# A DiT block on one core: summing a gate vector over partition quadrants by copies, and regrouping the K projection around its scale groups

## The chip, the core and the metric

The kernel runs on one core of one Trainium2 chip. The metric is the device time of one execution in microseconds; the time before is the median of five executions. A profile of one execution stands beside it. Engines are named as the profile names them: PE (matrix multiply), PEld (its weight loads), DVE (vector engine), ACT (scalar engine), POOL (GpSimd), SP (sync engine, which here only issues DMAs).

## The reference, cut to what matters

```python
B, N, D = x.shape            # 2, 256, 1152 ; F = 4 * D ; H = 2 heads of 576
mod = (_silu(c) @ w_mod).reshape(B, 6, 1, D)
shift_a, scale_a, gate_a, shift_m, scale_m, gate_m = [mod[:, i] for i in range(6)]
h = _layernorm(x, axis=-1) * (1 + scale_a) + shift_a
qkv = (h @ wqkv).reshape(B, N, 3, H, Dh)
# ... attention over 256 tokens, softmax, a = attention @ wo
x = x + gate_a * a
h2 = _layernorm(x, axis=-1) * (1 + scale_m) + shift_m
m = _gelu(h2 @ w_fc1) @ w_fc2
return x + gate_m * m
```

All inputs are bfloat16. Two pieces matter here: `1 + scale_a`, which multiplies the normalised x before the K projection, and `gate_m`, a vector of 1152 numbers for each of the two samples, which multiplies the result of the MLP at the very end.

## The kernel before, in words

The 512 tokens (`T`, two samples of `N` = 256) lie as four tiles of 128 rows. D = 1152 is nine blocks of 128 (`KD`), F = 4608 is 36 (`KF`). All matrix products accumulate in PSUM tiles with the tag "acc", of which there are six; smaller PSUM results use the tag "aux", of which there are two. Weights go through five large SBUF buffers (the pool "wide"), loaded by SP in the order in which the code names them. At the end of the program every instruction is chained to the one before it on its own engine (lines 820 to 830), so each engine executes exactly in the order in which the code is written; engines meet only through semaphores.

The parts that the change touches are these.

**The K projection, lines 376 to 410.** `k_step(k, c0, c1, m0, m1)` multiplies block k of the modulated input `hT0` with the weight blocks m0 to m1 - 1 of `w_k`, for token columns c0 to c1; six output blocks (`KM1`) accumulate side by side in the six "acc" tiles while k runs from 0 to 8. Steps 0, 1 and 2 are done in halves of 256 tokens, one half for each sample; steps 3 to 8 take all 512 columns in one matmul for each output block. Ahead of step k + 1, `transpose_x` turns block k + 1 of the normalised x with four PE transposes into an aux tile, and `both` multiplies it with the scale: DVE takes sample 0 (the first 256 columns), ACT takes sample 1 (the other 256). The scale itself comes from `scale_group(k0, k1)`: nine matmuls with two columns for each block, out of `w_scale_a`, which arrives by DMA in five pieces (`SGROUPS`: blocks 0-1, 2-3, 4-5, 6-7, 8), each followed by the piece of `w_k` that goes with it. The groups for blocks 4-5, 6-7 and 8 are computed inside steps 3, 5 and 7. In steps 3 and 5, `split` says how many of the six matmuls of the step are issued ahead of the scale group; the rest follow after the group and the transposes.

**The gate of the MLP.** `gate_vector(1, w_gate_m)` is called after output block m = 22 of the first MLP product (line 784). On DVE it multiplies each of the nine row blocks of the gate weights with the sample's silu(c), one number for each partition, and adds them up in `part` (lines 468 to 476). What remains is a sum over the 128 partitions. DVE's 32 x 32 block transpose and a reduction (lines 477 to 483) sum over the 32 partitions of each quadrant and leave `folded`: in quadrant a, partition 32a + r holds the quadrant's partial sums of columns 32j + r. `gate_vector_finish`, called after m = 34 (`KF - 2`, line 786), adds the four quadrants and turns the result: two matmuls in fp32 with the constant 0/1 matrix `fold` (built at line 454), one for each sample. DVE casts the 36 x 64 result to bfloat16, POOL writes it to DRAM (`gates_dram`, line 495), and `broadcast_gate` (line 460) reads it back into all 128 partitions as `gate`.

**The second MLP product, lines 800 to 817.** Thirteen groups, each 36 matmuls into an "acc" tile; DVE then multiplies with the gate (line 812, the first reader of `gate_m`), POOL adds x1, SP writes the rows out.

Of the kernel before, what the change touches and what calls it, by code (L numbers as in the profile page):

```python
# [8 lines left out]
FP32 = mybir.dt.float32  # L9
BF16 = mybir.dt.bfloat16  # L10
ACT = mybir.ActivationFunctionType
ALU = mybir.AluOpType
AX = mybir.AxisListType
# [6 lines left out]
def kernel(  # L20
# [11 lines left out]
    nc = tc.nc  # L32
    B, N, D = x.shape
# [3 lines left out]
    P = 128  # L37
    T = B * N
# [3 lines left out]
    KF = F // P  # L42
# [10 lines left out]
    const = ctx.enter_context(tc.tile_pool(name="const", bufs=1))  # L53
    act = ctx.enter_context(tc.tile_pool(name="act", bufs=1))
    wide = ctx.enter_context(tc.tile_pool(name="wide", bufs=5))
    work = ctx.enter_context(tc.tile_pool(name="work", bufs=2))
    small = ctx.enter_context(tc.tile_pool(name="small", bufs=4))
    psum = ctx.enter_context(tc.tile_pool(name="psum", bufs=2, space=PSUM))

    def acc_tile(shape, name, dt=FP32):  # L60
        return psum.tile(shape, dt, name=name, tag="acc", bufs=6)

    def aux_tile(shape, name, dt=FP32):
        return psum.tile(shape, dt, name=name, tag="aux", bufs=2)
# [27 lines left out]
    ident = const.tile([P, P], BF16, name="ident")  # L92
# [26 lines left out]
    def load_rows(name, view, col0):  # L119
        w = wide_tile(name)  # L120
        for r in range(0, KD, 3):
            load = nc.sync.dma_start(w[:, r:r + 3, :], view[:, r:r + 3, col0:col0 + D])
            first_load.setdefault(name, load.ins)
        return w
# [118 lines left out]
    def scale_group(k0, k1, tile_of=aux_tile, pm=None):  # L243
        if pm is None:
            pm = tile_of([P, k1 - k0, B], "pm")
        for j in range(k0, k1):
            if j == 0:
                nc.tensor.matmul(pm[:, 0, :], ones_row[:], ones_row[:, 0:B], start=True, stop=False)
            for k in range(KD):
                nc.tensor.matmul(  # L250
                    pm[:, j - k0, :], w_scale_a[:, k, j * P:(j + 1) * P], sT[:, k, 0:B],
                    start=(k == 0 and j > 0), stop=(k == KD - 1),
                )
        return pm

    def scale_add(pm, k0, k1, eng="d"):
        if eng == "a":
            nc.scalar.activation(scale_a[:, k0:k1, :], pm[:], ACT.Identity, bias=ones[:])
        else:
            nc.vector.tensor_scalar_add(scale_a[:, k0:k1, :], pm[:], 1.0)  # L260

    def transpose_x(ks, ts, pt=None, j0=0):
        if pt is None:
            pt = aux_tile([P, len(ks), len(ts) * P], "pt", BF16)
        for j, t in enumerate(ts, j0):
            for i, k in enumerate(ks):
                nc.tensor.transpose(pt[:, i, j * P:(j + 1) * P], xns[t][:, k * P:(k + 1) * P], ident[:])
        return pt
# [9 lines left out]
    def k_step(k, c0=0, c1=T, m0=0, m1=KM1):  # L278
        for m in range(m0, m1):
            if k == 0 and c0 == 0:  # L280
                pk[m] = acc_tile([P, T], "pk")
            nc.tensor.matmul(  # L282
                pk[m][:, c0:c1], w_k[:, k, m * P:(m + 1) * P], hT0[:, k, c0:c1],
                start=(k == 0 and c0 == 0), stop=(k == KD - 1), skip_group_check=True,
            )
# [33 lines left out]
    def both(pt, k):  # L319
        for b, e in enumerate("da"):  # L320
            modulate(pt, 0, k, b, b * N, e)
# [76 lines left out]
    k_step(2, 0, N)  # L398
    k_step(2, N, T)
    for k in range(3, KD):  # L400
        split = 2 if k in (3, 5) else 0
        k_step(k, 0, T, 0, split)
        if k in (3, 5, 7):
            k1 = min(k + 3, KD)
            scale_add(scale_group(k + 1, k1), k + 1, k1)
        if k < KD - 1:
            both(transpose_x([k + 1], range(NT)), k + 1)
        k_step(k, 0, T, split)
    for m in range(KM1):
        k_evac(m)  # L410

# [38 lines left out]

    s32 = const.tile([P, KD, B], FP32, name="s32")
    nc.vector.tensor_copy(s32[:], sT[:, :, 0:B])
    fold = const.tile([P, 32], FP32, name="fold")
    nc.vector.tensor_reduce(fold[:], ident[:].rearrange("p (q a) -> p a q", a=32), axis=AX.X, op=ALU.add)
    gates_dram = tc.dram_tile([2, B, D], BF16, name="gates_dram")

    def broadcast_gate(g):
        gate = act.tile([P, B, D], BF16, name="gate", tag="gate")
        for b in range(B):
            nc.gpsimd.dma_start(gate[:, b, :], gates_dram[g, b:b + 1, :].partition_broadcast(P))  # L460
        return gate
# [3 lines left out]
    def gate_vector(g, wg):  # L465
        part = act.tile([P, B, D], FP32, name="part", tag="x_sb")
        folded = small.tile([P, B, D // 32], FP32, name="folded", tag="folded", bufs=1)
        for k in range(KD):
            for b in range(B):
                if k == 0:  # L470
                    nc.vector.tensor_scalar_mul(part[:, b, :], wg[:, k, :], s32[:, k, b:b + 1])  # L471
                else:
                    nc.vector.scalar_tensor_tensor(  # L473
                        part[:, b, :], wg[:, k, :], s32[:, k, b:b + 1], part[:, b, :],
                        op0=ALU.mult, op1=ALU.add,
                    )
        for b in range(B):
            for c in range(0, D, PW):
                blocks = work.tile([P, PW // 32, 32], FP32, name="tmp", tag="tmp", bufs=3)
                nc.vector.transpose(blocks[:].rearrange("p j r -> p (j r)"), part[:, b, c:c + PW])  # L480
                nc.vector.tensor_reduce(
                    folded[:, b, c // 32:(c + PW) // 32], blocks[:], axis=AX.X, op=ALU.add
                )

        return lambda: gate_vector_finish(g, folded)

    def gate_vector_finish(g, folded):
        rows = D // 32
        pg = aux_tile([rows, B, 32], "pg")
        for b in range(B):  # L490
            nc.tensor.matmul(pg[:, b, :], folded[:, b, :], fold[:], start=True, stop=True)
        nat = work.tile([rows, B, 32], BF16, name="nat_v", tag="nat_v", bufs=1)
        nc.vector.tensor_copy(nat[:], pg[:])  # L493
        for b in range(B):
            nc.gpsimd.dma_start(gates_dram[g, b, :].rearrange("(j r) -> j r", r=32), nat[:, b, :])  # L495
        return broadcast_gate(g)

    def gate_natural(g, wg):
# [130 lines left out]
    w_gate_m = load_rows("w_gate_m", wmod_v, S_GATE_M * D)  # L629
# [106 lines left out]
    def load_f2(j):  # L736
        w = wide.tile([P, 27, PW], BF16, name=f"w_f2_{j}", tag="wide")
        i = 27 * j
        while i < 27 * (j + 1):
            n, kk = divmod(i, KF)  # L740
            cnt = min(KF - kk, 27 * (j + 1) - i)
            nc.sync.dma_start(w[:, i - 27 * j:i - 27 * j + cnt, :], wfc2_v[:, kk:kk + cnt, n * PW:(n + 1) * PW])
            i += cnt
        w_f2.append(w)
# [3 lines left out]
    def f1_mm(dst, m, k, c0, c1, start, **kw):  # L748
        ml = m % KD
        nc.tensor.matmul(  # L750
            dst, w_f1[m // KD][:, k, ml * P:(ml + 1) * P], hT[:, k, c0:c1],
            start=start, stop=(k == KD - 1), **kw,
        )
# [23 lines left out]
    gate_m = None  # L777
    for m in range(MSPLIT, KF):
        pacc = acc_tile([P, T], "pacc")
        for k in range(KD):  # L780
            f1_mm(pacc[:], m, k, 0, T, k == 0)
        nc.scalar.activation(gT[:, m, :], pacc[:], ACT.Gelu_apprx_tanh)  # L782
        if m == 22:
            gate_m_finish = gate_vector(1, w_gate_m)
        if m == KF - 2:
            gate_m = gate_m_finish()
        if m == MSPLIT:
            load_f2(0)
        if m > MSPLIT and m % KD == KD - 1:
            load_f2(m // KD)  # L790
# [9 lines left out]
    for gi, (n, t, c0, cw) in enumerate(groups):  # L800
        b = t // TPB
        last = gi == len(groups) - 1
        pacc = acc_tile([P, cw], "pacc")
        for kk in range(KF):
            j, r = divmod(n * KF + kk, 27)
# [3 lines left out]
                start=(kk == 0), stop=(kk == KF - 1),  # L809
# [51 lines left out]
```

## Time and profile before

| what | value |
|---|---|
| median of five executions | 243.68 us (243.43 to 244.09) |
| the profiled execution, its own time | 243.68 us |
| its span (first to last instruction in the profile) | 241.9 us |
| PE busy | 235.6 us, 97% of the span |
| DVE, ACT, POOL busy | 38%, 25%, 12% of the span |
| granted PE clock | 1.00 throughout |
| DMA traffic | 53.30 MB, mean 220 GB/s |

How to read it: a row of the chain of waits or of the timeline begins with the start in us from the start of the span and a length in us. "x18" is the number of instructions merged into the row. In the timeline the end of a matmul is modelled and includes the time in the pipeline, so the rows of PE overlap; a row of n matmuls that follow each other is as long as n - 1 distances from start to start and one duration. In the chain of waits the pieces do not overlap. A bracket at the end of a timeline row is the idle time of that engine just before, and what ended it. Time to landing of a DMA is counted from its issue.

### The profile page before, as it was taken

To read this page: it belongs to the slowest core of one execution; us is meant where nothing else is said; L and a number is where in the kernel's file an instruction comes from. 1 tells how busy PE (TensorE), PEld (TensorE's weight loads), DVE (VectorE), ACT (ScalarE), POOL (GpSimd) and SP (SyncE) were. 2 spreads that over 40 slices of the span, in tenths; PEclk is the share of its full clock that TensorE was granted. 3 is DMA by queue.
4 is the path that set the end of the run, shared out by engine and by line. 5 is a ranking of instruction groups with operands and counts; after the bars stand their busy time and mean duration, and the time that the engine had idled before them with its cause. 6 is when DMAs were issued, how large, how long until landed. Compare 5 with 4: busy or idle time off the path is not lost.

```text
span 241.9 us, 3993 instructions
## 1 busy us (share of the span) xinstructions
PE 235.6 (97%) x1698; PEld 144.1 (60%) x1698; DVE 91.5 (38%) x194; ACT 60.1 (25%) x122; POOL 28.3 (12%) x47
## 2 busy tenths in 40 slices
PE   8799999999999999999999999999999999999994
PEld 6575444466667666888844444444666566665674
DVE  4842442319325678831002999960010000000001
ACT  6732322307215032671422333322000000000000
POOL 2300000002300323200000000001121111111111
PEclk9999999999999999999999999999999999999999
DMA  6999999996599993739999999999300000000000
GB/s 213 327 315 310 377 366 392 390 391 224 106 327 394 390 290 76 194 60 354 390 390 393 340 327 289 265 326 294 98 16 16 20 16 16 19 18 16 25 26 16
DMA packets 48925, 53.30 MB, mean 220 GB/s; under 512 B 9731, under 2 KB 36619, under 8 KB 48907
## 3 DMA queue, kind: packets, MB, share of 16 engines
q1 hardware_dynamic: 41312, 50.14, 62.2%
q10 hardware_dynamic: 7083, 1.72, 4.4%
q0 software_dynamic: 512, 1.19, 1.9%
q8 instruction: 13, 0.21, 0.4%
q14 instruction: 5, 0.04, 0.1%
HBM read 50.15 MB, written 1.19 MB: 212 GB/s over the span
## 4 chain that ended last, share of the span: by engine, by line
PE 91%; SPq 4%; DMA 4%; issue 0%; DVE 0%; DVEq 0%
PE pacc L806 29%; PE pacc L750 29%; PE pacc L697 7%; PE pacc L603 7%; PE pq L525 7%; DMA w_scale_a<-in_w_mod_dram 4%; SPq L106 3%; PE pk L311 2%; PE pk L282 2%; PE pa L644 2%; PE ps_s L560 2%; PE pn L420 2%; SPq L88 1%; SPq L109 1%; PE pg L502 0%; PE pm L250 0%
## 5 line engine op out<-in xcount | busy, mean ns | idle before, releaser
L750 PE MATMUL pacc<-hT,w_f 128*128 128x256 bf16 (+1 forms) x432 | 70.5, 326 | 0.0
L806 PE MATMUL pacc<-w_f,gT 128*128 128x384 bf16 (+2 forms) x468 | 70.5, 314 | 0.0
L806 PEld LDWEIGHTS <-gT 128*128 128x128 bf16 x468 | 44.4, 98 | 26.3
L750 PEld LDWEIGHTS <-w_f 128*128 128x128 bf16 x432 | 42.2, 98 | 27.6
L812 DVE TENSOR_TENSOR tmp<-pacc,gate 128x384 f32<-128x384 f32 (+2 forms) x13 | 6.9, 527 | 65.6 <-PE pacc L806 57.1
L782 ACT ACTIVATE gT<-pacc 128x512 bf16<-128x512 f32 x24 | 14.3, 597 | 32.6 <-PE pacc L750 32.6
L473 DVE SCALAR_TENSOR_TENSOR part<-w_gate_m,s,part 128x1152 f32<-128x1152 bf16 x16 | 21.4, 1412 | 0.0
L814 POOL TENSOR_TENSOR o_sb<-tmp,x 128x384 bf16<-128x384 f32 (+1 forms) x12 | 11.7, 972 | 53.9 <-DVE tmp L812 53.9
L697 PE MATMUL pacc<-w_o,big 128*128 128x384 bf16 x108 | 17.9, 326 | 0.0
L525 PE MATMUL pq<-hT,w_q 128*128 128x512 bf16 x81 | 17.8, 379 | 0.0
L603 PE MATMUL pacc<-w_v,hT 128*128 128x384 bf16 x108 | 17.7, 326 | 0.0
L603 PEld LDWEIGHTS <-hT 128*128 128x128 bf16 x108 | 10.5, 98 | 7.1 <-issue 0.3
L697 PEld LDWEIGHTS <-big 128*128 128x128 bf16 x108 | 10.4, 98 | 7.2 <-issue 0.4
L525 PEld LDWEIGHTS <-w_q 128*128 128x128 bf16 x81 | 7.8, 98 | 9.4
L282 PE MATMUL pk<-big,w_k 128*128 128x256 bf16 (+1 forms) x72 | 13.2, 325 | 0.0
L703 POOL TENSOR_TENSOR x<-tmp,x_sb 128x384 f32<-128x384 f32 x8 | 7.3, 912 | 27.1 <-DMA w_scale_m<-in_w_mod_dram 15.2
L471 DVE TENSOR_SCALAR part<-w_gate_m,s 128x1152 f32<-128x1152 bf16 x2 | 1.6, 819 | 22.1 <-DMA w_gate_m<-in_w_mod_dram 22.1
L495 POOL DMA_DIRECT2D gates_dram<-nat_v x2 | 1.1, 534 | 67.7 <-DVE nat_v L493 67.7
L282 PEld LDWEIGHTS <-w_k 128*128 128x128 bf16 x72 | 6.8, 97 | 3.5 <-issue 0.2
L771 ACT ACTIVATE gT<-pacc 128x512 bf16<-128x512 f32 x12 | 6.5, 598 | 9.1 <-PE pacc L750 9.1
L516 POOL DMA_DIRECT2D gates_dram<-nat x4 | 2.3, 583 | 49.7 <-DVE nat L513 49.1
L702 DVE TENSOR_TENSOR tmp<-pacc,gate 128x384 f32<-128x384 f32 x12 | 6.6, 548 | 3.1 <-PE pacc L697 3.1
(106 smaller groups left out, 163.3 us busy)
## 6 DMA issues: line engine op xcount, KB each, us to landing
w_f<-in_w_fc_dram SPq DMA_DIRECT2D x12, 864.0 KB, 14.4
w_f<-in_w_fc_dram SPq DMA_DIRECT2D x3, 1728.0 KB, 10.0
w_f<-in_w_fc_dram SPq DMA_DIRECT2D x2, 2592.0 KB, 17.3
w_gate_a<-in_w_mod_dram SPq DMA_DIRECT2D x3, 864.0 KB, 12.7
w_v<-in_wqkv_dram SPq DMA_DIRECT2D x3, 864.0 KB, 13.8
w_o<-in_wo_dram SPq DMA_DIRECT2D x3, 864.0 KB, 14.0
w_shift_m<-in_w_mod_dram SPq DMA_DIRECT2D x3, 864.0 KB, 8.4
w_scale_m<-in_w_mod_dram SPq DMA_DIRECT2D x3, 864.0 KB, 14.8
```

The lines of the kernel that those rows point to most:

```text
L106: nc.sync.dma_start(w_k[:, k0:k1, c0:c1], wqkv_v[:, k0:k1, D + c0:D + c1])
L282: nc.tensor.matmul(pk[m][:, c0:c1], w_k[:, k, m * P:(m + 1) * P], hT0[:, k, c0:c1], start=(k == 0 and c0 == 0), stop=(k == KD - 1), skip_g ...
L473: nc.vector.scalar_tensor_tensor(part[:, b, :], wg[:, k, :], s32[:, k, b:b + 1], part[:, b, :], op0=ALU.mult, op1=ALU.add,)
L525: nc.tensor.matmul(pq[m][:], w_q[:, k, m * P:(m + 1) * P], hT[:, k, :], start=(k == 0), stop=(k == KD - 1), skip_group_check=True,)
L603: nc.tensor.matmul(pacc[:], hT[:, k, t * P:(t + 1) * P], w_v[:, k, pnl * PW:(pnl + 1) * PW], start=(k == 0), stop=(k == KD - 1),)
L697: nc.tensor.matmul(pacc[:], aT[:, k, t * P:(t + 1) * P], w_o[:, k, c0:c1], start=(k == 0), stop=(k == KD - 1),)
L703: (nc.gpsimd if pool_add else nc.vector).tensor_tensor(x1[:, t, c0:c1], tmp[:], x_sb[:, t, c0:c1], op=ALU.add)
L750: nc.tensor.matmul(dst, w_f1[m // KD][:, k, ml * P:(ml + 1) * P], hT[:, k, c0:c1], start=start, stop=(k == KD - 1), **kw,)
L782: nc.scalar.activation(gT[:, m, :], pacc[:], ACT.Gelu_apprx_tanh)
L806: nc.tensor.matmul(pacc[:], gT[:, kk, t * P:(t + 1) * P], w_f2[j][:, r, c0 - n * PW:c0 - n * PW + cw], start=(kk == 0), stop=(kk == KF - 1),)
L812: nc.vector.tensor_tensor(tmp[:], pacc[:], gate_m[:, b, c0:c0 + cw], op=ALU.mult)
L814: (nc.vector if last else nc.gpsimd).tensor_tensor(o_sb[:], tmp[:], x1[:, t, c0:c0 + cw], op=ALU.add)
```

## The change

Two parts of the code are changed.

In the K projection, three instead of two of the six matmuls of steps 3 and 5 are issued ahead of the scale group. Steps 4 and 6 are done in two halves of 256 columns, first the six matmuls of sample 0, then the six of sample 1.

In the gate of the MLP, the two fp32 matmuls with `fold` are gone, and so is `fold`. In their place POOL copies the four partition quadrants of `folded` by four DMAs from SBUF to SBUF side by side onto 32 partitions (`quads`); DVE sums the four with one reduction into `total`, a tile of 32 x 96 that is cleared first, turns it with a 32 x 32 block transpose, and casts it to bfloat16. Two DMAs write the result to DRAM, and the broadcast is as before. All of this is now issued in one go from `gate_vector` after m = 22; nothing is left after m = 34.

```diff
@@ K projection
     for k in range(3, KD):
-        split = 2 if k in (3, 5) else 0
+        split = 3 if k in (3, 5) else 0
         k_step(k, 0, T, 0, split)
         if k in (3, 5, 7):
             k1 = min(k + 3, KD)
             scale_add(scale_group(k + 1, k1), k + 1, k1)
         if k < KD - 1:
             both(transpose_x([k + 1], range(NT)), k + 1)
-        k_step(k, 0, T, split)
+        for c0, c1 in ((0, N), (N, T)) if k in (4, 6) else ((0, T),):
+            k_step(k, c0, c1, split)
...
-    fold = const.tile([P, 32], FP32, name="fold")
-    nc.vector.tensor_reduce(fold[:], ident[:].rearrange("p (q a) -> p a q", a=32), axis=AX.X, op=ALU.add)
...
@@ gate_vector
-        return lambda: gate_vector_finish(g, folded)
-
-    def gate_vector_finish(g, folded):
         rows = D // 32
-        pg = aux_tile([rows, B, 32], "pg")
-        for b in range(B):
-            nc.tensor.matmul(pg[:, b, :], folded[:, b, :], fold[:], start=True, stop=True)
-        nat = work.tile([rows, B, 32], BF16, name="nat_v", tag="nat_v", bufs=1)
-        nc.vector.tensor_copy(nat[:], pg[:])
-        for b in range(B):
-            nc.gpsimd.dma_start(gates_dram[g, b, :].rearrange("(j r) -> j r", r=32), nat[:, b, :])
+        quads = small.tile([32, P // 32, B * rows], FP32, name="quads", tag="quads", bufs=1)
+        for a in range(P // 32):
+            nc.gpsimd.dma_start(quads[:, a, :], folded[32 * a:32 * (a + 1), :, :].rearrange("p b j -> p (b j)"))
+        total = small.tile([32, 96], FP32, name="total", tag="total", bufs=1)
+        nc.vector.memset(total[:], 0.0)
+        nc.vector.tensor_reduce(
+            total[:, 0:B * rows], quads[:].rearrange("p a c -> p c a"), axis=AX.X, op=ALU.add,
+        )
+        turned = small.tile([32, 96], FP32, name="turned", tag="turned", bufs=1)
+        nc.vector.transpose(turned[:], total[:])
+        nat = small.tile([32, 96], BF16, name="nat_v", tag="nat_v", bufs=1)
+        nc.vector.tensor_copy(nat[:], turned[:])
+        flat = gates_dram[g, :, :].rearrange("b (j r) -> (b j) r", r=32)
+        nc.gpsimd.dma_start(
+            flat[0:64, :].rearrange("(q c) r -> c q r", q=2), nat[:, 0:64].rearrange("c (q r) -> c q r", q=2),
+        )
+        nc.gpsimd.dma_start(flat[64:B * rows, :], nat[0:B * rows - 64, 64:96])
         return broadcast_gate(g)
...
@@ first MLP product
         if m == 22:
-            gate_m_finish = gate_vector(1, w_gate_m)
-        if m == KF - 2:
-            gate_m = gate_m_finish()
+            gate_m = gate_vector(1, w_gate_m)
```

## Prediction

> **What bounds the kernel now.** I read the page first: which engine is busy, and what ended last.
>
> ```profile
> PE 235.6 (97%) x1698; PEld 144.1 (60%) x1698; DVE 91.5 (38%) x194; ACT 60.1 (25%) x122; POOL 28.3 (12%) x47
> ...
> PE 91%; SPq 4%; DMA 4%; issue 0%; DVE 0%; DVEq 0%
> ```
>
> PE makes up 91% of the chain that ended last, so an edit can pay only if it takes instructions off PE or shortens a stretch in which PE stands still. The other engines have more than half of their time free. Next I read the chain of waits in order of time, to see where it leaves PE.
>
> ```profile
> 10.98 8.70 DMA w_scale_a<-in_w_mod_dram
> 19.68 0.04 issue
> 19.73 0.60 PE pm L250 x18
> ...
> 21.44 0.22 PE pt L267 x4
> 21.66 1.34 PE pk L282 x6
> ...
> 97.95 68.26 PE pacc L750 x423
> 166.21 0.26 PE pg L491 x4
> 166.46 2.05 PE pacc L750 x9
> 168.51 70.31 PE pacc L806 x468
> ```
>
> Up to 19.68 us the end is set by SP's queue and one transfer: the piece of `w_scale_a` for blocks 6-7, issued at 10.98, landed 8.70 us later. From 19.73 on PE runs to the last groups with no piece of another engine in between. So a PE instruction saved after 19.73 moves the end by its full length, as long as no landing or release comes up behind it; PE time saved before 19.73 gains nothing, it only lengthens the wait there. The four `pg` pieces (two fp32 matmuls, executed as four passes) are on that chain. The waits of PE confirm the one late DMA:
>
> ```profile
> PE pm L250 <- DMA w_scale_a<-in_w_mod_dram: 0.6, 1, 0.6
> ```
>
> The timeline around this wait (step 5 with its group, then step 6), with one earlier row of half-width matmuls:
>
> ```profile
> 10.06 1.03 PE L282 MATMUL pk<-big,w_k 128*128 128x256 bf16 x8
> ...
> 17.27 1.89 PE L282 MATMUL pk<-big,w_k 128*128 128x512 bf16 x8
> ...
> 20.64 0.35 DVE L273 TENSOR_SCALAR big<-pt,scale_a 128x256 bf16<-128x256 bf16 x1
> ...
> 21.03 0.47 ACT L274 ACTIVATE big<-pt,scale_a 128x256 bf16<-128x256 bf16 x1 [2.75 <-DVE big L273]
> ...
> 21.28 0.39 PE L267 MATMUL pt<-ident,xn 128*128 128x128 bf16 x4
> ...
> 21.55 1.46 PE L282 MATMUL pk<-big,w_k 128*128 128x512 bf16 x6
> ```
>
> See three things. The eight matmuls from 17.27 start every (1.89 - 0.38)/7 = 0.216 us (0.38 is one duration), so PE is out of work at 17.27 + 8 x 0.216 = 19.00 and stands until 19.73: 0.73 us (the page counts 0.58, from the modelled end). ACT begins only when DVE has finished its half, and ends at 21.50. Step 6 starts at 21.55, 0.27 after the transposes before it, where other steps start 0.22 after theirs: about 0.05 us of waiting for ACT that the page does not list.
>
> Last, the timeline at the gate:
>
> ```profile
> 164.30 0.60 ACT L782 ACTIVATE gT<-pacc 128x512 bf16<-128x512 f32 x1 [1.34 <-PE pacc L750]
> 166.13 0.33 PE L491 MATMUL pg<-fold,folded 128*36 128x32 f32 x4
> 166.24 0.60 ACT L782 ACTIVATE gT<-pacc 128x512 bf16<-128x512 f32 x1 [1.35 <-PE pacc L750]
> ...
> 168.54 0.60 ACT L782 ACTIVATE gT<-pacc 128x512 bf16<-128x512 f32 x1 [1.71 <-PE pacc L750]
> 171.48 1.11 POOL L460 DMA_DIRECT2D gate<-gates_dram  x2 [3.41 <-DMA gates_dram<-nat_v]
> 175.24 0.56 DVE L812 TENSOR_TENSOR tmp<-pacc,gate 128x384 f32<-128x384 f32 x1 [8.53 <-DMA gate<-gates_dram]
> ```
>
> Gelu follows each output block, so its starts are a clock for PE: 1.94 us from block to block, but 2.30 us over the block with `pg` in front. The gate arrives at 175.24 and its first reader waits for it, without hurting PE.
>
> **The change part by part.**
>
> *The fp32 matmuls go.* By the clock of the gelus they cost 2.30 - 1.94 = 0.36 us of PE; by their pieces in the chain, 0.26. I take 0.36, since it also holds what the switch between data types costs around them. Nothing takes their place on PE. Gain 0.36.
>
> *The new path of the gate.* `folded` is done at 160.99 (the last reduction starts at 160.43 and takes 0.56). POOL followed DVE's cast by 0.29 us before, so the first copy is issued at 161.28; at 0.53 us for an issue (row of L495) the fourth goes at 162.87. The trace has no copy from SBUF to SBUF of this kind. The nearest row is the write of `nat_v`: 3.5 to 3.9 us to landing while weights stream; all DMAs with `gates_dram` lie between 1.6 and 5.2. I take 3.7, landing at 166.6. DVE then reduces 288 numbers (row of L481: 0.55 for 384), transposes 96 columns (L425: 0.32 for 128) and casts (0.22): about 1.1 with handover; the memset runs while the copies fly. At 167.7 + 0.29 = 168.0 POOL issues two writes, the second at 168.5, landing at 172.0 by 3.5; the broadcast is issued 0.43 later, as before, and the gate is there 3.76 after that: 176.2, one microsecond later than before. With 1.6 for both steps it would be 172, with 5.2 for those and the broadcast 181. Here a rule of the Trainium skill reads otherwise: "DMA: Bandwidth & Descriptors", Anatomy of one DMA, gives a DMA from POOL a fixed cost of about 2.0 us, most of it the wait for the write's receipt. By it the copies land at 164.9 and the writes 1.5 us sooner after their issue: an estimate of 173. Both cost nothing, because PE does not wait for the gate: six accumulators are there, a group takes 70.31/12 = 5.86 us, so the seventh group at 168.3 + 6 x 5.86 = 203.5 is the first that needs the accumulator of the first. The cover is 22 us beyond the slow bound; gone, each microsecond over it would cost one.
>
> *Queues that this is moved past.* Issued at m = 22 instead of 34, the path adds four POOL issues (2.1 us) to four that stay, and on DVE a memset, a reduction and a transpose. DVE has nothing of its own between 160.99 and the first product with the gate; what stands behind the new wait on DVE is the gate's own path and L812, which needs the gate anyway. POOL has nothing between 99.3 and its first addition behind L812. SP's loads of `w_fc2` wait for none of these; the last was issued at 154.6, ahead of the copies, which move 37 KB against megabytes. ACT gets nothing. The fold constant at 33.44 took DVE 0.36 us ahead of 4.76 us of idle time: 0.
>
> *Three matmuls ahead of the group.* In step 5 the ninth matmul fills 0.216 of the 0.73 us of standing still. The landing is not touched: up to it SP issues the same transfers, which wait for no engine. So the group starts at 19.73 as before, and 0.216 us less work stands behind it. Gain 0.216. It shrinks once the landing comes over 0.51 us sooner, is gone at 0.73, and stays 0.216 if the landing is late. In step 3 the same move only shifts work about, with the group's weights present: 0, ahead of the wait anyway.
>
> *The price: less cover for the scaling.* Three matmuls instead of four now stand between the transposes of block 6 and those of block 7. Block 7's transposes start at 20.41 + 3 x 0.216 = 21.06, and step 6 could start at 21.28; ACT ends at 21.50. Undivided, step 6 would lose the 0.216 just won. Divided, its first half needs only DVE's part, ready at 20.99 (0.29 of slack), and its second half starts at 21.28 + 6 x 0.109 = 21.93 (0.43 of slack to ACT). So nothing waits, and the old 0.05 goes too. Step 4 works alike, before the wait: 0.
>
> *Halving a step.* Half-width matmuls start every (1.03 - 0.27)/7 = 0.109 us in steps 0 and 1. Twelve of them take 1.31 against six at 0.216, 1.30: +0.01 to +0.02 in step 6. A rule of the Trainium skill speaks against this: "TensorE: Matmul & The Clock Gate", Back-to-back issue gap, says that in a real stream of weight loads and matmuls the spacing is set by both, and gives about 81 ns at 128 columns and 131 at 512. Linear between them, 256 columns would be about 98 ns (an estimate), and halving would cost 12 x 98 - 6 x 131 = 0.39 us for step 6, turning the gain of the K part into a loss of 0.12 (0.27 - 0.39), in all 243.4. The row decides: this stream is at 216 ns for 512 columns, so width sets the spacing, and the weight load of 98 ns still fits into 109. The other formula of that section, N/2.4 + 2.5 ns, gives 109.
>
> *Sum.* -0.36 - 0.216 - 0.05 + 0.02 = -0.61 us. The profiled execution took 243.68 us with a span of 241.9; the 1.78 outside stays. It equals the median of the five runs, so the sum stands against both: 243.1 us.
>
> *What comes next.* With PE earlier by 0.25 after step 6, landings get nearer: the piece for block 8 lands at 14.02 + 8.0 = 22.0, wanted at 22.63 before; the last panel of `w_k` at 17.05 + 8.2 = 25.25, wanted at 25.67; `w_shift_a` at 18.51 + 10.8 = 29.31, wanted at 29.86. The smallest slack is 0.42, so 0.17 is left.
>
> **The rivals.**
>
> *The K part is lost again (0.22).* The panel of `w_k` lands 0.17 us or more too late for the earlier PE, or the scale piece lands sooner than in the profiled run and there was no wait to fill. For it: the margin is thin and one execution is no average. Against it: the transfers come from one queue in order, so a late panel goes with a late scale piece. It leaves the 0.36: 243.3.
>
> *Less is gained at the gate (0.10).* Only 0.26 comes off, or the first group of the second product starts later for another reason; with the K part 243.2.
>
> *The halved steps are bound by their weight loads (0.08), slower.* One mechanism: in steps 4 and 6 the 98 ns load does not hide behind a 107 ns matmul, as the tiles now change twice as often. If load and matmul added up, 24 x 0.096 = 2.3 us would come on top, in part hidden in step 4 by the wait at 19.73 (0.73 - 0.216 = 0.51): -0.61 + 2.3 - 0.51 = +1.2, so 244.9. It decides from 0.61/12 = 0.05 us more for each matmul of step 6. Against it: steps 0 to 2 run in halves already, at 0.109.
>
> *The gate lands after 203 us:* slower too, but nothing in the trace is near to that; it has no share.
>
> **How the numbers follow.** 0.60 for the forecast at 243.1, with about 0.25 either way from run to run (the five runs span 0.66). A measurement of this kernel can tell about 0.2%, 0.49 us, from no change; faster therefore means under 243.19. Of the forecast's 0.60 about 0.50 falls there, of the case of the gate half, of the lost K part 0.07: 0.62. Slower is the share of the weight loads: 0.08. The rest, 0.30, is within 0.2%. The range goes from 242.7, the forecast less its scatter and a little, to 243.7, which takes in the lost K part at 243.3 with its own scatter and ends where the change would bring nothing; the weight loads lie outside.
>
> **What would show it.** Right: no `pg` matmuls, gelu starts 1.94 us apart up to the last; the row of nine matmuls ahead of the group in step 5 and a PE wait of about 0.4 as the page counts it; steps 4 and 6 as rows of twelve half-width matmuls 0.109 apart; the group after the DMA wait still at about 19.7, and the first panel matmul at about 25.6 instead of 25.88; the first product with the gate between 172 and 181 with no PE wait behind it. Wrong: a new wait of PE on ACT or DVE in steps 4 to 7, on `w_k` or `w_shift_a` after 22 us, or half-width matmuls spaced wider than 0.11.

## The result, and the profile after

The changed kernel takes 242.83 us in the median of 43 runs, the kernel before 243.52 us in the median of 80 runs made beside them. The ratio is 0.9975, with a 95% interval of 0.9967 to 0.9983: faster by 0.25%, or 0.6 us. The profiled execution took 242.55 us with a span of 240.8.

The page of the kernel after, the same two lines as before:

```profile
PE 235.0 (98%) x1706; PEld 145.1 (60%) x1706; DVE 92.2 (38%) x196; ACT 60.1 (25%) x122; POOL 30.4 (13%) x51
...
PE 95%; DVE 2%; DMA 1%; issue 0%; SPq 0%; DVEq 0%
```

PE executes eight instructions more (twelve more halves, four passes of fp32 fewer) and is busy 0.6 us less. SP's queue and the scale pieces are gone from the chain: in this execution the profile lists no wait of PE for weights. The chain of waits of the kernel after, in order of time:

```profile
17.43 1.96 PE pk L282 x15
19.39 0.43 PE pm L250 x18
19.82 0.24 PE pt L267 x4
20.07 0.65 PE pk L282 x3
20.71 0.22 PE pt L267 x4
20.94 1.31 PE pk L282 x12
...
97.19 70.20 PE pacc L756 x432
167.39 70.30 PE pacc L810 x468
```

The last row begins at 167.39 instead of 168.51, 1.12 us sooner. The first product of the MLP is one piece of 70.20 us now, where it was 68.26 + 0.26 + 2.05 with `pg` in between. The timeline of the K projection in the kernel after, the rows that answer to those of before:

```profile
17.27 2.12 PE L282 MATMUL pk<-big,w_k 128*128 128x256 bf16 x15
19.23 0.59 PE L250 MATMUL pm<-sT,w_scale_a 128*128 128x2 bf16 x18
...
20.55 0.39 PE L267 MATMUL pt<-ident,xn 128*128 128x128 bf16 x4
20.77 1.47 PE L282 MATMUL pk<-big,w_k 128*128 128x256 bf16 x12
...
25.12 4.05 PE L311 MATMUL pk<-big,w_k 128*128 128x512 bf16 x18
```

The row of 15 holds twelve halves of step 4 and three whole matmuls of step 5 (a merged row shows one form only). Step 6 starts 0.22 us after the transposes ahead of it, where it took 0.27 before. From the group of step 5 to the first matmul of panel 6 it takes 25.12 - 19.23 = 5.89 us, against 25.88 - 19.73 = 6.15 before.

And the timeline at the gate, in the kernel after:

```profile
163.54 0.60 ACT L788 ACTIVATE gT<-pacc 128x512 bf16<-128x512 f32 x1 [1.35 <-PE pacc L756]
165.48 0.60 ACT L788 ACTIVATE gT<-pacc 128x512 bf16<-128x512 f32 x1 [1.34 <-PE pacc L756]
...
167.42 0.60 ACT L788 ACTIVATE gT<-pacc 128x512 bf16<-128x512 f32 x1 [1.35 <-PE pacc L756]
167.66 0.63 DVE L490 TENSOR_REDUCE total<-quads 32x72 f32<-32x288 f32 x1 [7.29 <-DMA quads<-folded]
...
169.12 0.55 POOL L498 DMA_DIRECT2D gates_dram<-nat_v  x1 [6.54 <-DVE nat_v L496]
...
171.04 1.14 POOL L459 DMA_DIRECT2D gate<-gates_dram  x2 [0.86 <-DMA gates_dram<-nat_v]
174.95 0.56 DVE L816 TENSOR_TENSOR tmp<-pacc,gate 128x384 f32<-128x384 f32 x1 [6.12 <-DMA gate<-gates_dram]
```

Gelu is 1.94 us apart up to the last block: the 0.36 us is gone in full. The gate arrives at 174.95, practically when it did.

Between these two executions the time falls by 1.13 us (243.68 to 242.55), nearly twice what the medians say. 0.36 of the 1.12 us on PE is the gate. Of the 0.76 left, 0.26 is the stretch behind the group (6.15 to 5.89), and 0.50 is the start of the group (19.73 to 19.23). The latter is mostly chance: the scale piece for blocks 6-7 landed at 10.98 + 8.7 = 19.7 in the one execution and at 11.03 + 7.0 = 18.0 in the other, as the DMA issues after show (KB, then us to landing). It was issued before PE reached any changed instruction.

```profile
w_scale_a<-in_w_mod_dram SPq DMA_DIRECT2D x1, 576.0 KB, 7.0
```

How much of the K part is chance and how much is real is what the experiments had to settle.

### The profile page after: what moved, and what is told of

Its sections match the earlier page's. It is cut to its first block, busy times and chain, and to the rows that moved or that the text cites. A ratio compares the mean times of both kernels' runs of the same rounds, so it can differ in the third digit from the quotient of the medians.

```text
span 240.8 us, 4017 instructions
## 1 busy us (share of the span) xinstructions
PE 235.0 (98%) x1706; PEld 145.1 (60%) x1706; DVE 92.2 (38%) x196; ACT 60.1 (25%) x122; POOL 30.4 (13%) x51
## 4 chain that ended last, share of the span: by engine, by line
PE 95%; DVE 2%; DMA 1%; issue 0%; SPq 0%; DVEq 0%
PE pacc L810 29%; PE pacc L756 29%; PE pacc L703 7%; PE pacc L609 7%; PE pq L531 7%; PE pk L282 5%; PE pk L311 2%; PE pa L650 2%; PE ps_s L566 2%; PE pn L421 2%; DMA x_sb<-in_x_dram 1%; DVE stats L195 1%; PE pt L267 1%; PE pm L250 1%; PE pg L508 0%; DVE xn L235 0%
## 5 line engine op out<-in xcount | busy, mean ns | idle before, releaser
L487 POOL DMA_DIRECT2D quads<-folded x4 | 2.0, 508 | 62.0 <-DVE total L489 62.0
L282 PEld LDWEIGHTS <-w_k 128*128 128x128 bf16 x84 | 7.9, 97 | 2.5 <-issue 0.2
```

What stands on the lines that cost most here:

```text
L282: nc.tensor.matmul(pk[m][:, c0:c1], w_k[:, k, m * P:(m + 1) * P], hT0[:, k, c0:c1], start=(k == 0 and c0 == 0), stop=(k == KD - 1), skip_g ...
```

## The experiments

Theory: the gate is worth 0.36 us always; the K part is worth 0.25 where PE waits for the scale piece, and about 0.06 where it does not. Rivals: all of it comes from the gate; the K part is worth the same always; the K part is lost again at a later transfer. In a profile I measure the K part by PE alone, from the first matmul behind the last transposes of block 3 (13.05 in the kernel before, 13.11 after) to the first of panel 6: this takes out what the start of an execution adds. The start scatters by itself: over all profiles that first matmul lies between 13.00 and 13.62, and in five of them PE waited 0.15 to 0.42 us for the scale piece for blocks 0-1, ahead of any changed instruction.

### Each part alone

The new path of the gate, with the old loop of the K projection:

```diff
+        split = 2 if k in (3, 5) else 0      # and no halves in steps 4 and 6
```

> The kernel before with the new path of the gate alone; the K projection is untouched. My theory: the four passes of the fp32 matmuls cost PE 0.36 us and nothing takes their place, so the time is 0.36 us below before (ratio 0.9985) in every execution, and gelu starts stay 1.94 us apart up to the last. Rival (all the gain comes from the gate, through the transfers or the queues as well): 0.6 us below, ratio 0.9975. Rival (none of it reaches the end): ratio 1.000. The profile also shows one more sample of the landing of the scale piece for blocks 6-7: with the old split PE waits for it if it lands after about 19.0 us.

Measured: 243.05 us beside 243.34, ratio 0.9987 (0.9977 to 0.9998); gelu 1.94 us apart up to the last. The 0.9985 of the theory lies inside the interval; 0.9975 and 1.000 lie outside.

The new loop of the K projection, with the old gate (`fold`, its matmuls and the call after m = 34):

> The kernel before with the regrouped K projection alone; the gate keeps its fp32 matmuls. My theory (the gain hangs on the landing): 0.25 us less in an execution in which the scale piece for blocks 6-7 lands after 19.2 us, 0.06 us less (two short waits for ACT, less two halved steps) in one in which PE does not wait for it; the median between, 0.06 to 0.25, ratio 0.9990 to 0.9998. Rival (the gain is the same in all executions): 0.25, ratio 0.9990. Rival (halved steps cost by their weight loads): slower, ratio above 1.000.

Measured: 243.50 us beside 243.34, ratio 1.0006 (0.9997 to 1.0016): no gain to be seen. Its waits of PE say where it went:

```profile
PE pn L421 <- DMA w_shift_a<-in_w_mod_dram: 0.4, 1, 0.4
```

The chain of this profile has the transfer itself:

```profile
18.06 11.61 DMA w_shift_a<-in_w_mod_dram
```

It landed at 29.67; PE, at panel 6 by 25.29, was ready for it at about 29.3. In this execution the scale piece for blocks 6-7 had landed at 18.6, so the old loop would not have waited for it either, and would have been no more than about 0.1 us later at `w_shift_a`. The edit did not cause this wait; a late `w_shift_a` takes away what little the K part wins.

All three once more, side by side on another chip:

> The kernel after, on the same chip and in the same rounds as the gate alone and the K part alone, since the two parts were timed apart from the sum so far. My theory: 0.36 of the gate and 0.06 to 0.25 of the K part, ratio to before 0.9975 to 0.9983. Rival (the K part brings nothing in the median, because a later transfer takes the wait over): as the gate alone, 0.9985 to 0.9988.

> The gate's new path alone once more, beside the kernel after: ratio to before 0.9985 by my theory; 0.06 to 0.25 us slower than after, by the rival equal to it.

> The regrouped K projection alone once more. My theory: 0.06 to 0.25 us faster than before, ratio 0.9990 to 0.9998, with no wait of PE for a scale piece in the profile. Rival: within 0.05 us of before, and the profile shows PE waiting for another transfer (w_k or w_shift_a) behind step 5, as the first sample of this kernel did (0.38 us on w_shift_a at 29.72).

| kernel | median, us | ratio to before (243.50) | 95% interval |
|---|---|---|---|
| after | 242.68 | 0.9969 | 0.9956 to 0.9982 |
| gate alone | 243.43 | 0.9989 | 0.9976 to 1.0002 |
| K part alone | 243.39 | 0.9996 | 0.9987 to 1.0005 |

The whole repeats. The gate alone comes out at nearly the same ratio, though its interval now takes in 1. The K part alone is again too small to be told from nothing, and its profile again has PE waiting for `w_shift_a` (0.28 us). I had expected it to show no wait for a scale piece: there was none in step 5, but 0.42 us at the start, for blocks 0-1. The gate alone, profiled, shows what the K part is for: with the old loop PE waits for the scale piece.

```profile
20.39 0.60 PE L250 MATMUL pm<-sT,w_scale_a 128*128 128x2 bf16 x18 [0.67 <-DMA w_scale_a<-in_w_mod_dram]
```

### The scale piece made late

To make the wait likely in every execution, two transfers change places:

```diff
     for k0, k1 in SGROUPS:
+        if k0 == 6:
+            load_k(k0, k1, 0, KM1 * P)       # ahead of the scale piece, and not after it
         nc.sync.dma_start(w_scale_a[:, :, k0 * P:k1 * P], ...)
```

> The kernel before with two transfers exchanged: the piece of w_k for blocks 6-7 is loaded ahead of the scale piece for blocks 6-7, which therefore lands about 384 KB later, 1.2 us at the rate of that stretch. The profiles so far show the scale piece landing between 17.9 and 19.7 us; here it should land between 19 and 21, so PE waits for it in step 5 in every execution, 0.5 to 2 us. Against the kernel before: +0.3 to +1.5 us, ratio 1.001 to 1.006.

> The kernel after with the same two transfers exchanged, to be compared with the same exchange in the kernel before. My theory: with the wait there in every execution, the third matmul ahead of the group is worth its full 0.216 us and the halves save the wait for ACT in step 6 (0.05, less 0.02), so this one is 0.36 + 0.25 = 0.61 us faster than the exchanged kernel before. Rival (the K part is worth nothing even then, since the next transfers, the panel of w_k or w_shift_a, are waited for instead): 0.36 us faster. In the profile the group of step 5 starts at the landing in both, and from there to the first matmul of panel 6 it takes 6.15 us before and 5.90 us after.

Measured: 244.53 and 243.51 us, ratios to before 1.0062 (1.0041 to 1.0083) and 1.0008 (0.9995 to 1.0020). The timelines of the two, first before, then after, with the exchange in both:

```profile
20.06 0.60 PE L253 MATMUL pm<-sT,w_scale_a 128*128 128x2 bf16 x18 [0.61 <-DMA w_scale_a<-in_w_mod_dram]
...
26.21 4.05 PE L314 MATMUL pk<-big,w_k 128*128 128x512 bf16 x18
```

```profile
19.90 0.60 PE L253 MATMUL pm<-sT,w_scale_a 128*128 128x2 bf16 x18 [0.61 <-DMA w_scale_a<-in_w_mod_dram]
...
25.80 4.05 PE L314 MATMUL pk<-big,w_k 128*128 128x512 bf16 x18
```

From the landing to panel 6 it takes 6.15 us in the one and 5.90 in the other, to the hundredth what was expected: where the landing rules, the K part is worth 0.25. The medians are 1.0 us apart, and by the ratios 1.3, rather than 0.61. Together the two intervals leave about 0.6 us either way, so 0.61 lies at their edge: that the exchanged kernel after is the faster one is clear, by how much is not, and the wait was seen in one profile of each. Neither kernel waited for `w_shift_a`: they come to it at 30.19 and 29.78, where the kernel after came at 29.10.

### The parts of the K projection

Two matmuls ahead of the group, halves kept; and three ahead, steps 4 and 6 whole:

```diff
-        split = 3 if k in (3, 5) else 0
+        split = 2 if k in (3, 5) else 0
```

> The kernel after with two instead of three matmuls ahead of the scale groups of steps 3 and 5; the halves stay. My theory: where PE waits for the scale piece it is 0.216 us slower than after, where it does not wait it takes the same time as after: against before -0.40 to -0.42 us in either case (0.36 of the gate, 0.04 to 0.06 of the short waits), ratio 0.9983. Rival (the third matmul ahead is worth 0.216 always): 0.22 us slower than after in all executions.

```diff
-        for c0, c1 in ((0, N), (N, T)) if k in (4, 6) else ((0, T),):
-            k_step(k, c0, c1, split)
+        k_step(k, 0, T, split)
```

> The kernel after with steps 4 and 6 in one piece of 512 columns; three matmuls stay ahead of the groups. My theory: PE reaches steps 4 and 6 0.216 us sooner than before, and stands there until ACT has scaled its half: about 0.27 us of waiting in each of the two steps in place of 0.05. What the third matmul ahead wins is lost again: against before -0.36 us (the gate alone), where the scale piece is early +0.22 to +0.43 more than after. In the profile the transposes of the next block are followed by step 4 and step 6 after 0.45 us instead of 0.22. Rival (the halves do nothing; ACT is early enough): as after, ratio 0.9975.

Measured: 243.28 us, ratio 0.9994 (0.9984 to 1.0003), and 243.22, ratio 0.9999 (0.9991 to 1.0007). Neither expected time was met: both kernels hold the gate's 0.36 and should have been at 0.9983 to 0.9985. The profiles are clearer than the times. In the second, both steps stand; its timeline:

```profile
17.12 0.39 PE L267 MATMUL pt<-ident,xn 128*128 128x128 bf16 x4
...
17.61 0.59 PE L282 MATMUL pk<-big,w_k 128*128 128x512 bf16 x2
...
20.84 0.47 ACT L274 ACTIVATE big<-pt,scale_a 128x256 bf16<-128x256 bf16 x1 [2.43 <-DVE big L273]
20.87 0.39 PE L267 MATMUL pt<-ident,xn 128*128 128x128 bf16 x4
...
21.36 0.81 PE L282 MATMUL pk<-big,w_k 128*128 128x512 bf16 x3
```

Steps 4 and 6 follow their transposes after 0.49 us instead of 0.22, each waiting for ACT (20.84 + 0.47 = 21.31, then 0.05). That is 2 x 0.27 = 0.54 us. My expectation set against it what the third matmul ahead would win, but in this execution PE did not wait for the scale piece, so there was nothing to win: -0.36 + 0.54 less the 0.10 of the old waits in steps 4 and 6 is +0.08 us, a ratio of 1.0003, inside the interval. For the halves this settles it: without them the third matmul ahead is a loss where the scale piece is early, 12.51 us to panel 6 here against 12.08 in the one profile of the old loop in which PE waits for no weights (the four-fold passes, below: 13.09 to 25.17). Against that same 12.08 the kernel after takes 12.01, so without the wait the whole K part is worth 0.07. For the first kernel the profile has PE at panel 6 after 12.07 us, with no wait for the scale piece in step 5, as the theory has it. The 0.06 between 12.07 and 12.01 is nearly all a short wait in step 3: its scale piece, for blocks 4-5, landed at 15.64, and the group started at 15.69. Why its median is not nearer to the kernel after I cannot say beyond the width of the interval.

Four matmuls ahead of the group, in search of something better:

```diff
-        split = 3 if k in (3, 5) else 0
+        split = 4 if k in (3, 5) else 0
```

> The kernel after with four instead of three matmuls ahead of the scale groups of steps 3 and 5; steps 4 and 6 stay in halves. It looks for a version that beats both. My theory: in an execution in which PE still waits for a scale piece, another 0.216 us is filled; where it does not wait, nothing changes as long as the scaling keeps up: block 7's transposes start 0.43 us after step 5 resumes, step 6 could start at 0.65, and DVE's half is ready at about 0.63 with its handover, so 0 to 0.05 is lost. Ratio to after between 0.9993 and 1.0003. Rival (the shorter cover bites): step 6 starts 0.1 to 0.2 us later than the transposes allow in both steps, 0.2 to 0.4 slower than after.

Measured: 242.88 us, ratio to before 0.9978 (0.9968 to 0.9988), beside the 0.9969 of the kernel after; 12.02 us to panel 6 against 12.01, and no wait for a scale piece in step 5. Nothing lost and nothing won.

### The price of the passes

```diff
         for b in range(B):
-            nc.tensor.matmul(pg[:, b, :], folded[:, b, :], fold[:], start=True, stop=True)
+            for r in range(4):
+                nc.tensor.matmul(pg[:, b, :], folded[:, b, :], fold[:], start=(r == 0), stop=(r == 3))
```

> The kernel before with each of the two fp32 matmuls of the gate done four times into the same accumulator, so the sums come out four times as large: sixteen passes in place of four. It tells whether the 0.36 us is the passes or the change of data type around them. If the passes carry it all, 0.09 us each, the gelu behind them starts 1.94 + 16 x 0.09 = 3.38 us after the one before it. If a fixed part of 0.10 (0.36 less the 0.26 of the chain) is paid once and 0.065 for a pass, 1.94 + 0.10 + 1.04 = 3.08. If nearly all is fixed, about 2.4.

Measured once (243.39 us). Its timeline, around the sixteen passes:

```profile
165.42 0.74 PE L492 MATMUL pg<-fold,folded 128*36 128x32 f32 x16
165.53 0.60 ACT L783 ACTIVATE gT<-pacc 128x512 bf16<-128x512 f32 x1 [1.35 <-PE pacc L751]
...
168.25 0.60 ACT L783 ACTIVATE gT<-pacc 128x512 bf16<-128x512 f32 x1 [2.13 <-PE pacc L751]
```

Gelu to gelu is 2.72 us: sixteen passes cost 0.78, four cost 0.36. So, if every pass costs the same, a pass costs (0.78 - 0.36)/12 = 0.035 us, and 0.22 us is paid once for breaking into the stream. This lies between the second and the third guess; by this line through two points, most of what the change saved at the gate is the interruption, not the work.

### The cover of the gate taken away

```diff
-        for b in range(B):
+        for b in [b for r in range(8) for b in range(B)]:
             for c in range(0, D, PW):
                 blocks = ...
```

> The kernel after with the block transposes and reductions of the gate done eight times over (same values): 42 of them more, 0.53 us of DVE each counting starts, so folded is complete about 45 us later, at about 205, and the gate arrives at about 218. It tests the price that the cover hides: the accumulator of the first group is wanted by the seventh at about 202.5, so PE should stand from then until the first product with the gate, some 15 us, and the end moves out by about as much. If accumulators are no limit, nothing moves. The four copies are issued when no weights stream any more: if their 5.3 us to landing in the kernel after came from the weights on the same DMA engines, they land in about 2 us here; if it is the kind of the copy, in about 5.

Measured once: 259.39 us, beside 243.37 for the kernel before. Its waits of PE:

```profile
PE pacc L810 <- DVE tmp L816: 13.8, 1, 13.8
```

Its timeline from the copies on:

```profile
205.34 2.02 POOL L487 DMA_DIRECT2D quads<-folded  x4 [106.80 <-DVE total L489]
208.63 0.63 DVE L490 TENSOR_REDUCE total<-quads 32x72 f32<-32x288 f32 x1 [3.50 <-DMA quads<-folded]
...
215.67 1.49 DVE L816 TENSOR_TENSOR tmp<-pacc,gate 128x384 f32<-128x384 f32 x3 [5.88 <-DMA gate<-gates_dram]
216.29 8.88 PE L810 MATMUL pacc<-w_f,gT 128*128 128x384 bf16 x36 [13.81 <-DVE tmp L816]
```

And the stretch just behind the stop, from its busy times by stretch (PE, PEld, DVE, ACT and POOL, then granted clock, DMA share and GB/s):

```profile
216.30:222.00 5.70, 5.70 (x18) 2.59 (x18) 2.53 (x5) 0.00 (x0) 5.61 (x6) 0.50 0.22 70
```

PE stops at the seventh group, as worked out, until the first product with the gate frees an accumulator at 216.29. That is 13.8 us; more is in the last row: for 5.7 us after the stop the clock is granted at 0.50, and 18 matmuls take 5.70 us, 0.32 each instead of 0.163, 2.8 us lost. Together 16.6, which less the 0.6 that the kernel after is faster makes the 16.0 measured against the kernel before. So the accumulators are the limit, and the gate of the kernel after, at 174.95, is some 27 us inside of it.

The copies, issued here with no weights under way, land in 1.6 us (the chain of this profile). In the kernel after it was 5.3; the stretch around them there has a DMA share of 1.09 at 321 GB/s, and from 168 on next to none.

```profile
206.85 1.61 DMA quads<-folded
```

```profile
quads<-folded POOLq DMA_DIRECT2D x1, 9.0 KB, 5.3
...
160.50:168.00 7.50, 7.50 (x37) 3.50 (x36) 0.34 (x1) 2.37 (x4) 2.01 (x4) 1.00 1.09 321
168.00:171.00 3.00, 3.00 (x21) 1.80 (x19) 0.76 (x3) 0.02 (x1) 1.06 (x2) 1.00 0.05 9
```

It is the traffic, not the kind of the copy.

## Why the prediction was right

Foreseen were 243.1 us and 0.61 us less than before; measured were 242.83 and, by the ratio, 0.61 less. That the two agree to the hundredth is luck: the interval runs from 0.41 to 0.80, and one term of the sum, the wait in step 5, was put in as if it were there every time.

**The fp32 matmuls, 0.36: right,** in every profile with the new path, and by the time of the gate alone (0.9987 and 0.9989, about 0.3 us, the second not clear of nothing). The choice of the gelu clock over the pieces of the chain (0.26) was the right one, since the gelus hold the interruption in full and the chain's pieces only part of it.

**The new path costs nothing: right, by a cancellation.** I put the copies at 3.7 us to landing, with 5.2 as the far end; it was 5.3, outside. The reduction took 0.63 where I read 0.55 off a longer row. The writes took 1.6 instead of 3.5, after the weights had stopped (9 GB/s from 168 to 171, in the row above). The sum, 176.2 against 174.95, was off by 1.3 us, and the trace of before showed why it could not matter. The fixed 2.0 us of the Trainium skill ("DMA: Bandwidth & Descriptors", Anatomy of one DMA) lies between the two landings measured for the copies, 1.6 without traffic and 5.3 with it; neither it nor my row was near to the loaded case.

**Three matmuls ahead, 0.216, and the wait for ACT, 0.05: right in size, wrong in how often.** Where the landing rules, 6.15 us became 5.90. But I took the wait of one profiled execution as that of the kernel. Of the three kernels with the old loop and the transfers in their old order, profiled once each after the kernel before, one waited for the scale piece (the gate alone, second time) and two did not (the gate alone, first time, and the four-fold passes). Over the twelve profiles with the transfers in their old order the piece landed between 18.0 and 20.3 us; the old loop is out of work 5.95 us (19.00 - 13.05) behind the first matmul after block 3's transposes, and by this estimate would have waited in three of the twelve. At 0.25 in three and 0.07 in nine the K part comes to about 0.12, and the sum to about 0.48, which also lies in the interval. In step 5 of the kernel after there was no wait left, where I had put about 0.4 into what the profile would show. I had this as the condition on the landing, and as a rival; it should have been weighed in the sum. Step 3, which I put at nothing, also held a wait for its scale piece in two profiles with two matmuls ahead: 0.05 us in the first kernel of the parts above, 0.08 in the gate alone, first time.

**The halves: right.** Twelve take 20.77 to 22.08, 1.31 us, 0.109 each; whole steps would stand 0.27 us each for ACT. So the row was rightly preferred to the first rule of the Trainium skill ("TensorE: Matmul & The Clock Gate", Back-to-back issue gap), with its 131 ns for 512 columns, where this stream is at 216.

**What comes next: the right kind, the wrong transfer.** I named the last panel of `w_k` as the nearest landing, with 0.17 us left, by subtracting in one execution. It was `w_shift_a`, with more slack in that execution, that PE waited for in both profiles of the K part alone. The lost K part was a rival at 0.22, and for the K part by itself it is the better description, by the second of its two ways: the scale piece was early, and there was no wait to fill.

**What stays open:** the two parts alone, 0.9987 x 1.0006 and 0.9989 x 0.9996, come to 0.9993 and 0.9985, and the kernel after was at 0.9975 and 0.9969. Both times the whole gained about 0.4 us more than the parts together. One set of intervals alone is just wide enough for nothing to be there, but the two lie on the same side, and no trace shows a cause. So the K part's share of the median, between nothing and about half a microsecond, is not settled; that it is 0.25 where PE waits for the scale piece is shown in the one pair of profiles made for it.

## What to carry to other kernels

Read a wait on a transfer in several executions before you put its removal into a sum: landings here moved by up to 2.3 us from run to run, and an edit that hides such a wait is worth its full amount only in those where the wait is there, and only up to the landing that comes next. A few small matmuls of another data type in the middle of a dense stream can cost more by the interruption than by their work (here 0.22 of 0.36 us, by an estimate from two kernels); if the other engines are idle, let them do it, by however long a way, as long as a count of free accumulators says how late the result may be. When cover is taken from a producer, split the consumer so that it begins with the half that is ready first.

## What the runs showed of the hardware

Small copies from POOL's queue from SBUF to SBUF land in 1.6 us on idle DMA engines and in 5.3 us while weights stream at 321 GB/s. Sixteen fp32 passes of 32 columns inside the bfloat16 stream cost 0.78 us of PE, four cost 0.36. The same 576 KB scale piece, in the same order on one queue, landed between 18.0 and 20.3 us in twelve profiles. In the one execution with a late gate, after 14 us of standing still PE's clock was granted at 0.50 for 5.7 us, so that a stop of 13.8 us cost 16.6.
